# Soft-MoE over sigmoid attention on one core: the last six score units in halves of 224 queries, and attention's buffers in one tile

## Chip, cores and metric

One core of a Trainium2 chip runs the whole program. The metric is device microseconds from launch to end. Each number of a run is that of one execution; three executions of the kernel before were timed, and one more was profiled.

## What is computed

Attention with a sigmoid in place of the softmax, and then a mixture of experts in which every expert gets four "slots" that are soft mixtures of all tokens:

```
# q, k, v: (8, 12, 448, 64) fp32
attn = sigmoid(q @ k^T / 8 - log(448))
x = (attn @ v) as (3584, 768)          # tokens x model
logits = x @ phi                        # (3584, 32): 8 experts x 4 slots
d = softmax(logits, over the tokens);  slots = d^T @ x        # (32, 768)
slot_out[e] = relu(slots[e] @ w1[e]) @ w2[e]   # w1 (8,768,1024), w2 (8,1024,768)
out = softmax(logits, over the slots) @ slot_out               # (3584, 768)
```

The weights w1 and w2 are 50 MB, q, k and v 33 MB, the output 11 MB; all pass through one core's DMA.

## The kernel before

**Attention.** Two heads make a pair; there are 48 pairs, and their work is cut into 168 units (`seq`): for an even pair units (p, 0) to (p, 3), for an odd one (p, 0) to (p, 2). A unit (p, c) with c under 3 takes 128 keys; the unit (p, 3) takes the last 64 keys of p and of p+1. `score` (L267) writes the unit's scores of both heads, 128 x 2 x 448, into a PSUM tile `sc` (two banks, one for each head; two such tiles take turns) with TensorE (PE), and then ScalarE (ACT) takes the sigmoid of all 896 columns into one of three buffers `att` (L285). `weigh` (L295) multiplies V with it into the sums `av` (L318; for the last pair by two column parts, L293). In step i of the main loop (L606) PE gets `score` of unit i, then `weigh` of unit i - 2. `evac_a` (ACT, L321) and `evac_b` (DVE, L325) carry finished sums to x, `evac_last` (L327) those of the last pair, by two copies of DVE. PE, ACT, DVE and the DMA queue on SP each run their instructions in the order of the program, written out by hand; waits come from the tiles' uses.

**Loads.** SP's queue issues all loads. `load_qk`, `load_v`, `load_vl` bring a pair's Q and K, its V and the V of the odd 64 keys into buffers that must have come free. In between, `load` (L145) brings weights in units of 384 KB (128 x 768 fp32) into the places that `slots` (L108) lists. After attention's buffers come `wpe`, `wpx`, the tiles `wc1` to `wc6` of a second pool `wpb`, which lies where attention's buffers `qk`, `v` and `att` were, then `wpy`, and then the tiles `wa`, whose first contents PE has to read first (L190, the first product with w1).

**End of attention.** An ACT instruction on one element of the last sigmoid's buffer (L628, `dmx`) loads the table for exp early. PE computes the logits of the last pairs (L360), turns three pairs' x (L354), DVE and ACT take the last softmax (L499 to L509), PE sums the slots (L440; the first two of these sums read `wpy`), and then goes through w1 (L190) and w2 (L822); the output rows leave at the end.

Of the kernel before, what the change touches and what calls it, by code (L numbers as in the profile page):

```python
# [18 lines left out]
P = 128  # L19
NFK = 3  # L20
LAG = 2
PACE = 1.25
# [11 lines left out]
N_C = 6  # L34
# [34 lines left out]
def soft_moe_attention(ctx: ExitStack, tc: tile.TileContext, qk, v, vl, phi, w, wq, w8, wz, cst, out):  # L69
# [28 lines left out]
    state = {"next": 0, "ring": 0, "used": 0, "room": 0, "wpb": None, "n8": 0, "call": 0}  # L98
# [3 lines left out]
    wk = wpa.tile([P, UNIT + HALF], F32, name="wk")  # L102

# [4 lines left out]
    slots = wa_slots[:n1] + [(wpy, 0, 0, 2)] + wa_slots[n1:] + [(wpe, 0, 0, 4), (wpx, 0, 0, 2)]  # L108
    slots += [("wc", n, 0, 1) for n in range(1, N_C)] + [("wc", N_C, 0, 2), (wpy, 0, 2, 4)]
    slots += wa_slots + [(wpe, 0, 0, 4), (wpx, 0, 0, 2), (wpy, 0, 0, 4)] + wa_slots  # L110

    def ring_tile(size=1):
        while state["used"] + size > state["room"]:
            pool, n, used, room = slots[state["ring"]]
            state.update(ring=state["ring"] + 1, used=used, room=room)
            if pool == "wa":
                pool = wpa.tile([P, room * UNIT], F32, name=f"wa{n}")
            elif pool == "wc":
                pool = state["wpb"].tile([P, room * UNIT], F32, name=f"wc{n}")
# [9 lines left out]
    def load_half():  # L129
        state["wh"] = wk[:, UNIT:]  # L130
        nc.sync.dma_start(wk[:, UNIT:], wz[0][:, 0:HALF])

    def load_wk():
        utile[units[N_K]] = wk[:, 0:UNIT]
        nc.sync.dma_start(wk[:, 0:UNIT], w[N_K // 2][:, N_K % 2 * UNIT:(N_K % 2 + 1) * UNIT])
# [58 lines left out]
    with ExitStack() as actx:  # L194
        ap = actx.enter_context(tc.tile_pool(name="ap", bufs=1))

        kinds = {"qk": [P, QW], "v": [P, NFK, P], "att": [P, 2, S]}

        def hold(kind, n=""):
            if kind == "qk" and n == 0:  # L200
                return wk[:, 0:QW]
            return ap.tile(kinds[kind], F32, name=f"{kind}{n}")
# [53 lines left out]
        def load_v(p):  # L256
            if p < NP:
                t = get("v", p % 2)
                nc.sync.dma_start(t[:], v[p])
                vts[p] = t  # L260
# [6 lines left out]
        def score(u):  # L267
            p, c = u
            if u == seq[2]:
                sc = [ps_av.tile([P, 512], F32, name=f"av1{h}") for h in range(2)]  # L270
            else:
                tile2 = ps_sc.tile([P, 2, 512], F32, name="sc")
                sc = [tile2[:, h, :] for h in range(2)]
            for t in range(2):
                pt, k0 = (p, c * P + t * 64) if c < NFK else (p + t, NFK * P)
                for h, r in enumerate(heads):
                    nc.tensor.matmul(  # L277
                        sc[h][64 * t:64 * t + 64, 0:S], qkts[pt][r, S + k0:S + k0 + 64], qkts[pt][r, 0:S],
                        start=True, stop=True)
            att = get("att", seq.index(u) % 3)  # L280
            if u == seq[2]:
                for h in range(2):
                    nc.scalar.activation(att[:, h, :], sc[h][:, 0:S], AF.Sigmoid, bias=nbias, scale=QSCALE)
            else:
                nc.scalar.activation(att[:], tile2[:, :, 0:S], AF.Sigmoid, bias=nbias, scale=QSCALE)  # L285
            atts[u] = att

        parts = (slice(0, 2 * P), slice(2 * P, S))

        def weigh_half(o, w, att, start, stop):  # L290
            for k, t in enumerate(parts):
                for h, r in enumerate(heads):
                    nc.tensor.matmul(o[k][r, 0:t.stop - t.start], w[:, r], att[:, h, t], start=start, stop=stop)  # L293

        def weigh(u):  # L295
# [6 lines left out]
            if p == NP - 1:  # L302
                weigh_half(avs[p], vts[p][:, c, :], att, False, c == NFK - 1)
                return
            for t in range(2):
                row = slice(64 * t, 64 * t + 64)
                if c == NFK and p + t == NP - 1:
                    weigh_half(avs[p + t], vls[p // 2][row, :], att[row], True, False)
                    continue
# [17 lines left out]
        def evac_last(p):  # L327
            x, av = x_of(p), avs.pop(p)
            for k, t in enumerate(parts):
                nc.vector.tensor_copy(x[:, t], av[k][:, 0:t.stop - t.start])  # L330
# [153 lines left out]
        def last_job(b, lgt, pw, px):  # L484
# [8 lines left out]
            for c0 in (0, 2):  # L493
                logits(lg, b, [NPR - 1], (0, 1, 2, 3), c0, c0 + 2)
# [110 lines left out]
        for i in range(len(seq) + LAG):  # L605
            for f in early.get(i, ()):  # L606
                f()
            if i < len(seq):
                u = seq[i]
                score(u)  # L610
# [12 lines left out]
            if i == len(seq) - 1:  # L623
                lgt = ps_sc.tile([P, 2, 512], F32, name="sc")
                keep(1, lgt)
                logits_old(lgt[:, 0, :])
# [4 lines left out]
            if i >= LAG:  # L631
                u = seq[i - LAG]
                weigh(u)
                p, c = u
                if c == NFK:
                    evac_b(p)
                    load_vl(p // 2 + 1)
                elif c == NFK - 1:
                    load_v(p + 2)
                    if p == NP - 1:  # L640
                        work(B * S)
                        pw = ps_av.tile([P, 512], F32, name="av00")
                        px = [ps_av.tile([P, 512], F32, name="av01")]
                        pxt = ps_sc.tile([P, 2, 512], F32, name="sc")
                        keep(0, pxt)
                        px += [pxt[:, 0, :], ps_av.tile([P, 512], F32, name="av10")]
                        continue
                    evac_a(p)
                    if p == NP - 3:
                        todo.append((0.65, lambda p=p: evac_b(p)))  # L650
                    elif p % 2 == 1:
                        evac_b(p)
            for f in late.get(i, ()):
                f()
            work(rate.get(i, PACE))
        finish, ph0 = last_job(B - 1, lgt, pw, px)

    state["wpb"] = ctx.enter_context(tc.tile_pool(name="wpb", bufs=1, reuse_waits="tile"))
# [86 lines left out]
    def combine_turn(n, c4):  # L745
# [8 lines left out]
        while at0 < t0 + nt:  # L754
            i, m = divmod(at0, UNIT)
            w = min(UNIT - m, t0 + nt - at0)
            if m == 0:
                cts[i] = state["wpb"].tile([P, UNIT], F32R, name=f"wc{i + 1}")[:]
# [76 lines left out]
    wc_last = state["wpb"].tile([P, 2 * UNIT], F32R, name=f"wc{N_C}")[:]  # L835
# [83 lines left out]
```

## Time and profile before

| | us |
|---|---|
| median of three runs | 369.77 (369.0 to 369.96) |
| the profiled execution's own time | 370.01 |
| its span (first to last instruction) | 368.2 |
| PE busy in the span | 347.4 (94%) |
| ACT, DVE busy | 222.5 (60%), 242.3 (66%) |

Moved by DMA: 95.21 MB. The time of a run lies some 2 us above the span. A busy time is a union: matmuls that overlap in the array count once. The profile's chain of waits goes back from the last instruction, at each step to what released it; the views in time order show when one instruction starts, how long it takes and how many of its kind follow each other (an fp32 matmul shows as two records). Times within the span are counted from its start.

### The profile page before, as it was taken

To read this page: it belongs to the slowest core of one execution; us is meant where nothing else is said; L and a number is where in the kernel's file an instruction comes from. 1 tells how busy PE (TensorE), PEld (TensorE's weight loads), DVE (VectorE), ACT (ScalarE), POOL (GpSimd) and SP (SyncE) were. 2 spreads that over 40 slices of the span, in tenths; PEclk is the share of its full clock that TensorE was granted. 3 is DMA by queue.
4 is the path that set the end of the run, shared out by engine and by line. 5 is a ranking of instruction groups with operands and counts; after the bars stand their busy time and mean duration, and the time that the engine had idled before them with its cause. 6 is when DMAs were issued, how large, how long until landed. Compare 5 with 4: busy or idle time off the path is not lost.

```text
span 368.2 us, 10407 instructions
## 1 busy us (share of the span) xinstructions
PE 347.4 (94%) x4341; PEld 177.0 (48%) x4341; DVE 242.3 (66%) x621; ACT 222.5 (60%) x307; POOL 10.1 (3%) x45
## 2 busy tenths in 40 slices
PE   9999999999999999999999999999999999699840
PEld 5666666644444446444444644464546553243620
DVE  0148829796795886869958695979955784123650
ACT  5777777577777774777777387758582114322640
POOL 1000000000000000000000000010103001000000
PEclk9999999999999999999999999999999999989985
DMA  6766666465676663666666387729899999999997
GB/s 216 228 211 206 195 225 203 157 215 173 209 228 214 200 189 113 217 210 208 196 215 209 101 280 259 271 72 350 292 334 349 417 441 426 411 426 402 384 412 281
DMA packets 34783, 95.21 MB, mean 259 GB/s; under 512 B 3632, under 2 KB 17584, under 8 KB 33328
## 3 DMA queue, kind: packets, MB, share of 16 engines
q1 hardware_dynamic: 34736, 94.55, 73.0%
q8 instruction: 34, 0.56, 0.6%
q14 instruction: 13, 0.11, 0.1%
HBM read 83.53 MB, written 11.01 MB: 257 GB/s over the span
## 4 chain that ended last, share of the span: by engine, by line
PE 80%; DMA 14%; DVE 2%; ACT 0%; issue 0%; ACTq 0%; DVEq 0%; SPq 0%
PE sc L277 35%; PE av L318 34%; DMA wpe<-in_wq_dram 9%; DMA wa<-in_w_dram 5%; PE sc L440 2%; PE av L190 2%; PE sc L378 2%; DVE wa L769 1%; PE av L768 1%; PE sc L360 1%; PE av L557 1%; PE pt L768 1%; PE av L293 1%; PE av L822 0%; PE av L440 0%
## 5 line engine op out<-in xcount | busy, mean ns | idle before, releaser
L285 ACT ACTIVATE att<-sc,sm 128x896 f32<-128x896 f32 x167 | 167.7, 1007 | 76.8 <-PE sc L277 73.6
L318 PE MATMUL av<-att,v 64*64 64x448 f32 x1128 | 140.3, 536 | 0.0
L277 PE MATMUL sc<-qk 64*64 64x448 f32 x896 | 118.4, 537 | 0.0
L318 PEld LDWEIGHTS av<-att,v 64*64 64x64 f32 x1128 | 51.0, 133 | 55.9 <-issue 46.3
L277 PEld LDWEIGHTS sc<-qk 64*64 64x64 f32 x896 | 41.7, 133 | 43.6 <-issue 29.6
L277 PE MATMUL sc<-wk 64*64 64x448 f32 x440 | 62.4, 546 | 0.0
L342 DVE STREAM_TRANSPOSE wa<-wpe 32x384 f32<-32x384 f32 (+5 forms) x144 | 58.0, 403 | 2.2
L342 DVE STREAM_TRANSPOSE wa<-xy 32x192 f32<-32x192 f32 (+3 forms) x96 | 33.1, 345 | 1.6
L325 DVE TENSOR_TENSOR wpe<-wpe,av 128x448 f32<-128x448 f32 x18 | 11.2, 621 | 31.8 <-PE av L318 20.6
L277 PEld LDWEIGHTS sc<-wk 64*64 64x64 f32 x440 | 21.3, 136 | 21.5 <-issue 15.1
L342 DVE STREAM_TRANSPOSE wa<-wpx 32x288 f32<-32x288 f32 (+1 forms) x48 | 24.9, 520 | 0.8
L822 PE MATMUL av<-wa,hw 128*32 128x384 f32 x208 | 21.1, 507 | 3.6 <-DMA wa<-in_w_dram 3.6
L318 PE MATMUL av<-att,wk 64*64 64x448 f32 x188 | 23.9, 536 | 0.0
L325 DVE TENSOR_TENSOR wpx<-wpx,av 128x448 f32<-128x448 f32 x15 | 9.3, 621 | 18.0 <-PE av L318 15.7
L190 PE MATMUL av<-wa,phi 128*32 128x256 f32 x312 | 17.6, 380 | 0.4 <-DVE phi L522 0.4
L325 DVE TENSOR_TENSOR xy<-xy,av 128x448 f32<-128x448 f32 x14 | 8.7, 622 | 9.4 <-ACT xy L321 3.8
L769 DVE COPY wa<-pt 128x384 f32<-128x384 f32 x23 | 11.9, 555 | 3.2 <-PE pt L768 2.8
L769 ACT COPY wa<-av 128x384 f32<-128x384 f32 x23 | 10.6, 479 | 4.7 <-PE av L768 4.0
L318 PEld LDWEIGHTS av<-att,wk 64*64 64x64 f32 x188 | 8.7, 133 | 9.5 <-issue 8.0
L190 PEld LDWEIGHTS av<-wa,phi 128*32 128x32 f32 x312 | 9.6, 110 | 7.3 <-DVE tmp L712 0.9
L715 ACT COPY t<-tmp 128x32 f32<-128x32 f32 x8 | 1.7, 218 | 17.5 <-DVE tmp L713 17.5
L342 DVE STREAM_TRANSPOSE wpe<-xy 32x256 f32<-32x256 f32 (+3 forms) x32 | 11.0, 344 | 0.5
(189 smaller groups left out, 287.2 us busy)
## 6 DMA issues: line engine op xcount, KB each, us to landing
wa<-in_w_dram SPq DMA_DIRECT2D x52, 384.0 KB, 4.1
qk<-in_qk_dram SPq DMA_DIRECT2D x32, 448.0 KB, 3.7
v<-in_v_dram SPq DMA_DIRECT2D x48, 192.0 KB, 2.6
wa<-in_wq_dram SPq DMA_DIRECT2D x6, 1536.0 KB, 31.3
wa<-in_w_dram SPq DMA_DIRECT2D x3, 3072.0 KB, 23.0
wk<-in_qk_dram SPq DMA_DIRECT2D x15, 448.0 KB, 3.4
out_dram<-wa SPq DMA_DIRECT2D x13, 384.0 KB, 7.4
out_dram<-wa SPq DMA_DIRECT2D x2, 1536.0 KB, 7.6
```

What stands on the lines that cost most here:

```text
L190: nc.tensor.matmul(ph[32 * j:32 * j + 32, 0:256], phi_sb[:, kc, :], wt, start=(kc == 0), stop=(kc == NKC - 1))
L277: nc.tensor.matmul(sc[h][64 * t:64 * t + 64, 0:S], qkts[pt][r, S + k0:S + k0 + 64], qkts[pt][r, 0:S], start=True, stop=True)
L285: nc.scalar.activation(att[:], tile2[:, :, 0:S], AF.Sigmoid, bias=nbias, scale=QSCALE)
L293: nc.tensor.matmul(o[k][r, 0:t.stop - t.start], w[:, r], att[:, h, t], start=start, stop=stop)
L318: nc.tensor.matmul(o[t][r, 0:S], w, att[row, h, :], start=start, stop=stop)
L325: nc.vector.tensor_tensor(out=x_of(p), in0=x_of(p), in1=av[0][:, 0:S], op=ALU.add)
L342: nc.vector.transpose(y[32 * g:32 * g + 32, k0:k0 + n, c0:c0 + m, BLK * a:BLK * a + BLK], src)
L378: nc.tensor.matmul(lg[32 * j:32 * j + 32, BLK * c0[j]:BLK * (c0[j] + n)], phi_sb[:, hp, :], blocks(x, j if x is xa else (j + 2) % 4, n), s ...
L440: nc.tensor.matmul(sls[t][32 * a:32 * a + 32, BLK * k0:BLK * k1], zt[:, c * BLK:(c + 1) * BLK], y_of(t, gi, c)[:, k0:k1, BLK * a:BLK * a + ...
L768: nc.tensor.matmul(pf[:, 0:HALF], ct_of(m, t, n), sts[hf], start=True, stop=True)
L769: (nc.scalar.copy, nc.vector.tensor_copy)[k % 2](ov, pf[:, 0:HALF])
L822: nc.tensor.matmul(po[32 * fl:32 * fl + 32, 0:HALF], h[:, k:k + NSLOT], w2_chunk(hf, e, g, fl), start=(n == 0), stop=(n == 2 * E - 1))
```

## The change

- The last six units, (46, 1) to (47, 2), go by halves of 224 queries. Half j = 2m or 2m + 1 belongs to unit m of these six. `score_half` writes both halves of a unit into one PSUM tile `sc`, columns 0:224 and 224:448 of each head's bank, and takes one sigmoid for each half, 128 x 2 x 224, into one of three buffers of 448 columns (`halves`) in place of 896. `weigh_half` uses one half. In a step PE now gets score 2m, weigh 2m - 2, score 2m + 1, weigh 2m - 1.
- All of attention's buffers but `qk0` and the last sums lie at written-out places in one tile `big` (7 units and 128 columns), and the weights that were in `wc1` to `wc6` go there by units, in the order 0, 3, (wpx), 1, 2, 6, 5, 4. The tile of two units, `wc6`, becomes two loads.
- V of the last two pairs goes into `xy`, to the columns where these pairs' x is put later. The V of the odd keys moves from `wk` into `big`, and the half unit of `load_half` is loaded with `load_wk`, eight places earlier in SP's queue.
- `evac_last` gives the second 224 columns to ACT in place of DVE, and the logits of the last pair are cut to fit.

```diff
+        halves = [big[:, a:a + S].rearrange("p (h s) -> p h s", h=2) for a in (at_att0 + S, at_att0, at_att1 + S)]
...
+                if p >= NP - 2:
+                    a = (p % 2 + 1) * NBK * P
+                    t = xy[:, a:a + nv].rearrange("p (c f) -> p c f", c=NFK)
+                nc.sync.dma_start(t, v[p])
...
+        parts = (slice(0, S // 2), slice(S // 2, S))
+        sc_half = [None]
+
+        def score_half(j):
+            (p, c), k = seq[len(seq) - N_HALF + j // 2], j % 2
+            if k == 0:
+                sc_half[0] = ps_sc.tile([P, 2, 512], F32, name="sc")
+            sc = sc_half[0][:, :, parts[k]]
+            for t in range(2):
+                pt, k0 = (p, c * P + t * 64) if c < NFK else (p + t, NFK * P)
                 for h, r in enumerate(heads):
+                    nc.tensor.matmul(
+                        sc[64 * t:64 * t + 64, h, :], qkts[pt][r, S + k0:S + k0 + 64], qkts[pt][r, parts[k]],
+                        start=True, stop=True)
+            nc.scalar.activation(halves[j % 3], sc, AF.Sigmoid, bias=nbias, scale=QSCALE)
...
-            for k, t in enumerate(parts):
-                nc.vector.tensor_copy(x[:, t], av[k][:, 0:t.stop - t.start])
+            for k, copy in enumerate((nc.vector.tensor_copy, nc.scalar.copy)):
+                copy(x[:, parts[k]], av[k][:, 0:S // 2])
...
-            if i == len(seq):
-                nc.scalar.activation(dmx[0:1, :], atts[seq[-1]][0:1, 0, 0:1], AF.Exp)
+            else:
+                nc.scalar.activation(dmx[0:1, :], halves[(2 * N_HALF - 1) % 3][0:1, 0, 0:1], AF.Exp)
...
+            if i > n0:
+                weigh_half(2 * (i - n0) - 2)
+                if i < len(seq):
+                    score_half(2 * (i - n0) + 1)
...
+                weigh_half(2 * (i - n0) - 1)
+                weighed(seq[i - 1])
+            elif i >= LAG:
+                weigh(seq[i - LAG])
+                weighed(seq[i - LAG])
+                if i == n0:
+                    score_half(1)
+                    weigh(seq[i - 1])
+                    weighed(seq[i - 1])
...
-    for k, size in enumerate((1, 1, 1, 1, 1, 1, 1, 2, 2)):
-        if k == N_C + 1:
+    for k, size in enumerate((1, 1, 1, 1, 1, 1, 1, 1, 1, 2)):
+        if k == 7:
             load_kept()
-        if k == 4:
-            load_half()
         load(size)
```

PE, the last units of attention, before: scores are L277, weighing L293, `Activation` in brackets is a wait for ACT.

```order
L277 MATMUL sc<-qk_3035 64x448 [waits Activation_49]
L277 MATMUL sc<-qk_3035 64x448 x3
L293 MATMUL av_3231<-att_3217,v_3178 64x256 [waits DMAHW3_49]
L293 MATMUL av_3231<-att_3217,v_3178 64x256
L293 MATMUL av_3232<-att_3217,v_3178 64x192 x2
L293 MATMUL av_3231<-att_3229,v_3178 64x256 [waits Activation_49]
```

The same place now: scores are L303, weighing L315.

```order
L303 MATMUL sc<-big 64x224 [waits PE_49]
L303 MATMUL sc<-big 64x224 x3
L315 MATMUL av_3002<-big,xy 64x224 x2
L303 MATMUL sc<-big 64x224 [waits Activation_49]
L303 MATMUL sc<-big 64x224 x3
L315 MATMUL av_3003<-big,xy 64x224 x2
L315 MATMUL av_3002<-big,xy 64x224 x2
L315 MATMUL av_3003<-big,xy 64x224 [waits Activation_49]
```

Of each unit the second half's scores wait for ACT, and the weighing that follows them needs no wait of its own. Before, the score of a unit waited for the sigmoid of the unit two steps back. In the built program the wait of the second half's first matmul has the count of one certain ACT instruction: the sigmoid of the same unit's first half.

ACT at the end of attention, before: L285 is the sigmoid, L628 the early exp, L501 belongs to the last softmax.

```order
L285 ACTIVATE att_3245<-sc,sm 128x896 [waits PE_49,Activation_49]
L628 ACT_TABLE_LOAD
L628 ACTIVATE sm<-att_3245 1x1 [waits Activation_49]
L501 COPY sm<-sm 32x1 [waits DVE_49,Pool_49]
L504 COPY sm<-sm 32x1 [waits DVE_49]
```

And now: L306 is a half's sigmoid, L358 the copy of `evac_last`.

```order
L349 COPY xy<-av_2945 128x448 [waits DMAHW6_49,PE_49]
L306 ACTIVATE big<-sc,sm 128x448 [waits PE_49,Activation_49] x6
L670 ACT_TABLE_LOAD
L670 ACTIVATE sm<-big 1x1 [waits Activation_49]
L358 COPY xy<-av_3003 128x224 [waits DMAHW4_49,DVE_49,PE_49]
L530 COPY sm<-sm 32x1 [waits DVE_49,Pool_49]
```

The copy of the last sums to x stands on ACT, behind the table load, which stands behind the last half's sigmoid.

SP's queue from the second load of `wpe` on, before.

```order
L172 DMA wpe<-in_w_dram 128x1536 [waits DVE_49,DMAHW2_49,PE_49,Pool_49]
L259 DMA v_3178<-in_v_dram 128x384 [waits DMAHW3_49,PE_49]
L172 DMA wpx<-in_w_dram 128x768 [waits DMAHW4_49,DVE_49]
L172 DMA wpx<-in_w_dram 128x768 [waits DMAHW5_49]
L172 DMA wc_3413<-in_w_dram 128x768 [waits DMAHW6_49,PE_49]
L172 DMA wc_3415<-in_w_dram 128x768 [waits DMAHW7_49,PE_49]
```

And now, from the same place to `wpy`.

```order
L169 DMA wpe<-in_w_dram 128x1536 [waits DVE_49,DMAHW3_49,PE_49,Pool_49]
L263 DMA xy<-in_v_dram 128x384 [waits DMAHW4_49]
L169 DMA big<-in_w_dram 128x768 [waits DMAHW5_49,PE_49]
L169 DMA big<-in_w_dram 128x768 [waits DMAHW6_49,PE_49,Activation_49]
L169 DMA wpx<-in_w_dram 128x768 [waits DMAHW7_49,DVE_49]
L169 DMA wpx<-in_w_dram 128x768 [waits DMAHW0_49]
L169 DMA big<-in_w_dram 128x768 [waits DMAHW1_49,PE_49]
L169 DMA big<-in_w_dram 128x768 [waits DMAHW2_49]
L169 DMA big<-in_w_dram 128x768 [waits DMAHW3_49,PE_49]
L127 DMA lt<-in_wz_dram 128x768 [waits DMAHW4_49,DVE_49]
L169 DMA big<-in_w_dram 128x768 [waits DMAHW5_49,PE_49,Activation_49]
L169 DMA big<-in_w_dram 128x768 [waits DMAHW6_49,PE_49,Activation_49]
```

V of the last pair no longer waits for PE, and two weight units stand ahead of `wpx`. The next row in both is the load of `wpy`, which waits for PE and GpSimd (POOL) in both; what has been loaded by then is the same set.

## Rows read from the trace of the kernel before

**Rows 1.** The chain of waits, in order of time: start us, us, what.

```profile
288.48 18.28 DMA wa<-in_w_dram
...
306.82 33.15 DMA wpe<-in_wq_dram
...
341.71 0.49 ACT tmp L795
...
342.25 0.61 PE av L806 x2
```

**Rows 2.** Busy time by stretches: us, engines, granted clock, DMA share, GB/s.

```profile
264.00:276.00 12.00, 12.00 (x132) 5.76 (x131) 7.72 (x20) 8.87 (x10) 1.30 (x5) 1.00 0.90 308
276.00:280.00 4.00, 3.90 (x116) 3.28 (x112) 2.73 (x13) 2.43 (x10) 1.57 (x6) 1.00 0.94 305
...
288.00:300.00 12.00, 12.00 (x224) 6.82 (x220) 9.92 (x38) 1.86 (x8) 0.21 (x1) 1.00 1.03 434
310.00:320.00 10.00, 7.84 (x73) 2.96 (x73) 2.26 (x8) 4.67 (x12) 0.84 (x4) 1.00 0.98 415
320.00:325.00 5.00, 3.56 (x22) 1.42 (x22) 1.12 (x2) 0.59 (x2) 0.21 (x1) 0.78 1.01 423
```

**Rows 3.** SP's queue in time order, 263 to 286 us: start, us, issue.

```profile
263.89 0.83 SPq L172 DMA_DIRECT2D wpe<-in_w_dram  x2
267.17 0.33 SPq L259 DMA_DIRECT2D v<-in_v_dram  x1
...
276.55 0.51 SPq L172 DMA_DIRECT2D wc<-in_w_dram  x1
280.12 0.33 SPq L172 DMA_DIRECT2D wpy<-in_w_dram  x1
280.71 1.58 SPq L168 DMA_DIRECT2D wa<-in_wq_dram  x3
284.15 1.62 SPq L172 DMA_DIRECT2D wa<-in_wq_dram  x2
```

**Rows 4.** DMA issues of the page: count, KB each, median us from issue to landing.

```profile
wk<-in_vl_dram SPq DMA_DIRECT2D x24, 64.0 KB, 2.2
wpe<-in_w_dram SPq DMA_DIRECT2D x2, 768.0 KB, 4.7
...
wpy<-in_w_dram SPq DMA_DIRECT2D x1, 768.0 KB, 6.7
```

**Rows 5.** PE in time order, 265 to 277 us: start, us, matmuls.

```profile
265.43 0.93 PE L277 MATMUL sc<-qk 64*64 64x448 f32 x8
266.18 0.93 PE L318 MATMUL av<-att,v 64*64 64x448 f32 x8
...
272.63 0.50 PE L293 MATMUL av<-att,wk 64*64 64x192 f32 x4
272.94 0.94 PE L277 MATMUL sc<-qk 64*64 64x448 f32 x8
273.81 2.49 PE L293 MATMUL av<-att,v 128*64 128x256 f32 x24
```

**Rows 6.** ACT in time order, 266 to 277 us.

```profile
266.49 1.01 ACT L285 ACTIVATE att<-sc,sm 128x896 f32<-128x896 f32 x1 [0.50 <-PE sc L277]
...
274.00 1.01 ACT L285 ACTIVATE att<-sc,sm 128x896 f32<-128x896 f32 x1 [0.50 <-PE sc L277]
275.03 1.28 ACT L628 ACT_TABLE_LOAD   x1
276.32 0.20 ACT L628 ACTIVATE sm<-att 1x1 f32<-1x1 f32 x1
```

**Rows 7.** ACT line 283, the two sigmoids of 448 columns near the start: min/median/max ns.

```profile
L283 ACT ACTIVATE att<-av,sm x2: 634/638/642, 7.3 to 7.8; 128x448 f32<-128x448 f32 x2
```

**Rows 8.** DVE in time order, 275 to 280 us.

```profile
276.02 0.69 DVE L330 COPY xy<-av 128x256 f32<-128x256 f32 x2 [0.19 <-PE av L293]
277.19 0.29 DVE L499 CUSTOM_DVE_ANT_0 t<-sc,t 128x128 f32<-128x128 f32 x1 [0.47 <-PE sc L360]
```

More of the change, by code (lines that the diff above doesn't have):

```diff
@@ L21 @@
 LAG = 2
+N_HALF = 6
 PACE = 1.25
@@ L97, in soft_moe_attention @@
     N_SEQ = len(units) - 2
-    state = {"next": 0, "ring": 0, "used": 0, "room": 0, "wpb": None, "n8": 0, "call": 0}
+    state = {"next": 0, "ring": 0, "used": 0, "room": 0, "n8": 0, "call": 0}
     utile, quads = {}, {}
@@ L107, in soft_moe_attention @@
     n1 = 3 + (n1 - 3) // 2
-    slots = wa_slots[:n1] + [(wpy, 0, 0, 2)] + wa_slots[n1:] + [(wpe, 0, 0, 4), (wpx, 0, 0, 2)]
-    slots += [("wc", n, 0, 1) for n in range(1, N_C)] + [("wc", N_C, 0, 2), (wpy, 0, 2, 4)]
+    slots = wa_slots[:n1] + [(wpy, 0, 0, 2)] + wa_slots[n1:] + [(wpe, 0, 0, 4), (big, 0, 0, 1), (big, 0, 3, 4)]
+    slots += [(wpx, 0, 0, 2)] + [(big, 0, n, n + 1) for n in (1, 2, 6, 5, 4)] + [(wpy, 0, 2, 4)]
     slots += wa_slots + [(wpe, 0, 0, 4), (wpx, 0, 0, 2), (wpy, 0, 0, 4)] + wa_slots
@@ new lines, in weigh_half @@
+        def weigh_half(j):
+            (p, c), k = seq[len(seq) - N_HALF + j // 2], j % 2
+            att, q = halves[j % 3], parts[k]
+            if c == NFK and k == 0:
+                avs[p + 1] = [ps_av.tile([P, 512], F32, name=f"av1{t}") for t in range(2)]
+            if p == NP - 1:
+                for h, r in enumerate(heads):
+                    nc.tensor.matmul(
+                        avs[p][k][r, 0:S // 2], vts[p][:, c, r], att[:, h, :], start=False, stop=c == NFK - 1)
+                return
+            for t in range(2):
+                row = slice(64 * t, 64 * t + 64)
+                for h, r in enumerate(heads):
+                    if c < NFK:
+                        o, w, stop = avs[p][t][r, q], vts[p][row, c, r], c == NFK - 1 and t == k == 1
+                    elif t == 0:
+                        o, w, stop = avs[p][0][r, q], vls[p // 2][row, r], k == 1
+                    else:
+                        o, w, stop = avs[p + 1][k][r, 0:S // 2], vls[p // 2][row, r], False
+                    nc.tensor.matmul(o, w, att[row, h, :], start=c == NFK and t == 1, stop=stop)
@@ L603, in work, with weighed @@
                 n -= k
-        for i in range(len(seq) + LAG):
+        def weighed(u):
+            p, c = u
+            if c == NFK:
+                evac_b(p)
+                load_vl(p // 2 + 1)
+            elif c == NFK - 1 and p < NP - 1:
+                load_v(p + 2)
+                evac_a(p)
+                if p == NP - 3:
+                    todo.append((0.65, lambda p=p: evac_b(p)))
+                elif p % 2 == 1:
+                    evac_b(p)
+        n0 = len(seq) - N_HALF
+        for i in range(len(seq) + 1):
             for f in early.get(i, ()):
@@ L609, in soft_moe_attention @@
                 u = seq[i]
-                score(u)
+                if i < n0:
+                    score(u)
+                else:
+                    score_half(2 * (i - n0))
                 if u[1] == NFK:
@@ L833, in soft_moe_attention @@
     h_part(*prev)
[L835 removed]
+    big = big_at(F32R)
+    wc_last = big[:, 5 * UNIT:7 * UNIT]
     c4s = {}
```

95 lines of the change are left out of this document (35 added, 60 removed).

## The prediction

> **What bounds the kernel now.** I read the chain of waits first. From 288.48 us to 339.97 us it is nothing but two transfers of weights, 18.28 and 33.15 us from issue to landing [rows 1]: the end is set by the DMA. The stretches show where that begins [rows 2]. From 288 to 300 us the share is 1.03 at 434 GB/s, and at 310 to 325 us still 415 to 423. From 264 to 276 us it is 0.90 at 308 GB/s, and PE is busy for the whole of it. So from somewhere past 280 us on the chip moves bytes as fast as they go, and the time is set by how many are left then and by whether the stream breaks. Ahead of that the loads wait for buffers.
>
> SP's queue says for which [rows 3]. The loads of `wpe` to `wc6` go out from 263.89 to 276.55 us, 14 of them, 5760 KB (5.90 MB). Then SP waits to 280.12 us, until PE has read `wpy` for the last time in the slot sums; the loads into `wa` behind it follow PE at 280.71 and 284.15 us. In 264 to 280 us 4.92 MB went (12 x 308 and 4 x 305), so some 0.98 MB were still queued when `wpy` came. This cushion is why the 3.5 us without an issue cost nothing. Whatever moves the issue of `wpy` by more than the cushion breaks the stream, and everything behind it is late.
>
> **What the change does on PE.** The columns stay the same, and so does array time: the part of unit (46, 3) that was already in 256 and 192 columns fits the usual rhythm, 272.63 to the next score at 272.94 us [rows 5]; more weight loads cost nothing there, and I take nothing. What is new is a wait. The order shows that the scores of a unit's second half wait for ACT, and the built program says for which instruction: the sigmoid of the first half, just ahead. Before, PE waited for a sigmoid two units back.
>
> The price of one such wait, from S, the start of the first half's scores:
> - a score of a unit holds PE for 0.75 us (265.43 to 266.18) and ends after 0.93, so its tail is 0.18 [rows 5]; a half issues for 0.375 and ends at S + 0.555;
> - the sigmoid began at 266.49, 0.13 after the scores ended at 266.36 [rows 5, 6]: S + 0.685;
> - a sigmoid of 448 columns took 0.638 us [rows 7], 896 took 1.01 [rows 6]: it ends at S + 1.32;
> - PE followed ACT after 0.05 us at 342.20 to 342.25 [rows 1]: S + 1.37.
>
> Between the two halves PE has one weighing of a half, so without the wait it would go on at S + 0.75. The loss is 0.62 us in each of five units, 3.1 us. In the first of the six a whole weighing (0.75) stands between, so it loses 0.25. The last weighing waits for the last sigmoid behind two halves of weighing, another 0.25. The sums of pair 46 are copied by ACT ahead of a sigmoid, 0.1 (estimate: the copy starts 0.31 after a half's scores do and holds ACT some 0.4, against 0.685). Sum 3.7 us. Bounds: with the sigmoid at half of 1.01 and half the lag of 0.13, the half scores' answer is at S + 1.17, the loss 0.42 for five and 0.05 for two, 2.2 us; with a half's sigmoid as dear as a whole one it is 1.0 and 0.6, 6.2 us. I stay with 3.7, because its row has the very size.
>
> **The end of attention.** Before, the last sigmoid ended at 275.01, the table load ran under PE's weighing until 276.31, and DVE copied the last sums 276.02 to 276.71 [rows 6, 8]; the weighing ended at 276.30 [rows 5], so x was whole 0.41 us behind it. Now the last sigmoid ends only 0.60 us ahead of the end of weighing (0.05, then 0.375 and 0.18), and ACT's queue is sigmoid, table load 1.28, exp 0.20, copy. With 0.35 for the copy (half of DVE's 0.69) and 0.03 of gaps x is whole 1.86 us behind the sigmoid, 1.26 behind the weighing. That is 0.85 us later; the chain from there through DVE's step at 277.19 to the slot sums has the same links. Bounds 0.6 and 1.1. The Trainium skill (ScalarE: Activation LUTs, What ACT_TABLE_LOAD costs) gives the load 1.28 us and a drain of 1.38 us behind it; the row has the 1.28, but the exp began 0.01 us after it, so the trace shows no drain here. By the page this term would be 2.2 and the whole change 1.4 us dearer.
>
> **What comes earlier.** V of pair 47 need not wait for 267.17 any more, and four units of weights can start in 267 to 271 us, where three of them stood among the loads up to 276.55. This fills gaps (share 0.90). But `wpy` stands behind them, all loads ahead of it are the same bytes, and they are through before it comes, so the early start is worth only what it takes out of the cushion, and only if `wpy` is not late. The one load more (`wc6` in two) and the moves of V and the half unit in SP's queue are costed at nothing: the queue is waiting, not issuing, there. The first 162 units wait for the same things as before.
>
> **The sum.** `wpy` is released 3.7 + 0.85 = 4.55 us later. The cushion takes part of it. `wpy` landed 6.7 us after its issue, `wpe` of the same size 4.7 [rows 4]: by this it stood 2.0 us behind others. By bytes 0.98 MB at about 0.41 is 2.4 us, less the time that a transfer needs to begin, which lies between 0 and the 2.2 us of a 64 KB load [rows 4]: 0.2 to 2.4. I take 1.6, nearer to the landings. The stream breaks for 4.55 - 1.6 = 2.95 us. Behind it nothing gives this back, since the share is 0.98 to 1.03 there [rows 2]. Nor is more lost: `wpy` and the three `wa` loads behind it (2304 KB, some 5.7 us) keep the stream full from about 286 to 291.9 us, and the next two `wa` loads come at 284.15 + 4.55 = 288.7 [rows 3]; and PE, 1.6 us later against the stream than before, has 2.16 us of idle time in 310 to 320 and 1.44 us in 320 to 325 [rows 2]. The profiled execution took 370.01, 0.24 above the median of 369.77; on its own time the sum is 372.96. I forecast 372.7 for the median.
>
> **The rivals.**
> - *The early loads decide, faster.* If PE's wait were hidden (its place: the second half's scores; ACT fast enough, or the wait not in the way), `wpy` would be 0.85 late, less than the cushion, and with all earlier bytes through, the stream gains 1.6 - 0.85 = 0.75 us: 369.0; with the copy hidden too, 368.2. It decides for a gain as soon as `wpy` comes less than 1.6 us late. For it: the share of 0.90. Against: the wait stands in the order, and 1.37 cannot go into 0.75. Chance 0.13, more than half of it beyond 0.3% (1.1 us, about what a measurement of this kernel can tell from no change).
> - *The wait is short and the cushion long, no change.* 2.2 + 0.6 - 2.4 = 0.4: 370.2. Against it is the row of 0.638 us. Chance 0.12.
> - *The clock falls.* The halved units keep PE busy 1.5 of 2.12 us, 71%. In 320 to 325 us PE was busy 3.56 of 5 us, 71%, and the granted clock was 0.78, between the levels; in 310 to 320 us it was busy 78% at 1.00 [rows 2]. At half clock a unit's PE work takes 3.0 us, and with a wait left of some 0.25, 3.25 instead of 2.12: over three units 3.4 us more, 376.1. The Trainium skill (TensorE: Matmul & The Clock Gate, Part 1: The HAM clock gate) says that the array's clock is halved when PE has been idle; which gaps did it in 320 to 325 no row here tells apart. Gaps of 0.6 us are short, so chance 0.07.
> - *Doesn't do what it says.* The order shows both halves and the new places; none of this is in doubt.
>
> **The numbers.** Forecast case 0.68; its own ends are 370.2 (2.2 + 0.6 less 2.4) and 374.5, where a wait of 0.75 makes 4.5 of 3.7, the copy is 1.1 and the cushion 0.9. Range 370.1 to 374.5: it leaves out the faster rival and most of the clock's. Slower by over 0.3%: 0.68 + 0.07 + 0.02 = 0.77; within: 0.05 from the first rival and 0.10 from the second, 0.15; faster 0.08.
>
> **What would show it.** PE at 266 to 280 us: idle ahead of every second half's scores, ended by ACT, 0.5 to 0.65 us in five units, and weighing ending near 280.0 instead of 276.30. ACT: table load behind the last half's sigmoid, the copy ending 1.2 to 1.3 us behind the weighing. SP: `wpy` issued near 284.7 instead of 280.12, and landing after 4.5 to 5 us instead of 6.7. The share of the DMA low (0.4 to 0.8) somewhere in 276 to 286 us, and as before from 290 on. I am wrong if PE does not wait there, or if it does and the stream does not break because more is queued than I count, or if weighing slows by itself under the doubled weight loads.

## The result, and the profile after

The changed kernel takes **373.97 us** (median of five runs, 373.33 to 374.35) beside 369.77 for the kernel before on the same chip: ratio 1.0108, 95% interval 1.0079 to 1.0138. It is slower, by 4.2 us; the forecast was 372.7 in a range of 370.1 to 374.5. Of the runs further down, two executions, of 928.24 and 525.09 us, are left out of the medians.

The two profiled executions are compared from one row that the change doesn't touch, the first of the two loads into `wpe`: 263.89 us before [rows 3], 264.38 after. What lies ahead of it differs by some tenths from one execution to the next (263.76 in a second profile of the changed kernel), so "later" below means later against that row, 0.49 us less than the plain difference of times.

The stretches say where the time went: span of the stretch, busy time of PE, PEld, DVE, ACT and POOL, granted clock, DMA share, GB/s. First the kernel before, over stretches that its rows above did not group like this:

```profile
264.00:288.00 24.00, 23.50 (x394) 13.67 (x397) 15.03 (x52) 12.02 (x22) 4.58 (x17) 1.00 0.94 333
...
300.00:325.00 25.00, 21.40 (x231) 8.86 (x227) 10.26 (x35) 8.53 (x24) 1.88 (x9) 0.96 1.00 423
```

The same view after, first in whole and then the part that matters in pieces of 2 us:

```profile
264.00:288.00 24.00, 21.04 (x388) 12.10 (x378) 12.12 (x40) 13.11 (x26) 2.72 (x11) 1.00 0.76 268
288.00:300.00 12.00, 11.96 (x218) 7.05 (x218) 9.11 (x33) 1.65 (x7) 2.07 (x8) 1.00 1.02 409
300.00:325.00 25.00, 23.08 (x309) 10.53 (x301) 13.50 (x50) 8.79 (x26) 1.69 (x8) 1.00 1.00 426
...
276.00:278.00 2.00, 1.71 (x24) 0.61 (x20) 0.12 (x1) 1.18 (x2) 0.00 (x0) 1.00 0.44 173
278.00:280.00 2.00, 1.72 (x24) 0.73 (x18) 1.24 (x5) 0.80 (x2) 0.00 (x0) 1.00 0.00 0
280.00:282.00 2.00, 1.91 (x36) 0.89 (x32) 1.02 (x2) 1.97 (x4) 0.00 (x0) 1.00 0.57 147
282.00:284.00 2.00, 1.74 (x22) 1.65 (x23) 0.96 (x6) 0.82 (x4) 0.36 (x2) 1.00 0.68 204
284.00:286.00 2.00, 1.92 (x81) 1.38 (x83) 1.62 (x8) 1.31 (x6) 0.94 (x3) 1.00 0.95 363
286.00:288.00 2.00, 1.64 (x52) 1.07 (x44) 0.87 (x5) 0.00 (x0) 0.12 (x1) 1.00 0.78 274
```

From 264 to 288 us the DMA's share fell from 0.94 to 0.76, 4.3 us of transfers in 24; from 288 us on it is full as it was [rows 2]. The loss is a hole in the stream of weights, and it lies wholly in this stretch. The hole has two parts: from 276 to 284 us the shares leave 4.6 us of transfers unused (nothing at all moves from 278 to 280), and there is a smaller gap of 0.4 us at 286. PE, idle for 0.5 us of the stretch before, now idles 3.0.

PE in time order shows why. L303 is the scores of a half, L327 and L315 the weighing of a half (L315 is the last pair); columns are start, us, line, operation, shape, count, and in brackets the idle time ahead and what ended it:

```profile
265.91 0.56 PE L303 MATMUL sc<-big 64*64 64x224 f32 x8
...
267.28 0.61 PE L303 MATMUL sc<-big 64*64 64x224 f32 x8
...
268.46 0.56 PE L303 MATMUL sc<-big 64*64 64x224 f32 x8
268.84 0.56 PE L327 MATMUL av<-big,xy 64*64 64x224 f32 x8
269.83 0.61 PE L303 MATMUL sc<-big 64*64 64x224 f32 x8 [0.44 <-ACT big L306]
270.26 0.56 PE L327 MATMUL av<-big,xy 64*64 64x224 f32 x8
270.64 0.56 PE L303 MATMUL sc<-big 64*64 64x224 f32 x8
...
275.23 0.56 PE L303 MATMUL sc<-big 64*64 64x224 f32 x8
275.72 0.60 PE L315 MATMUL av<-big,xy 128*64 128x224 f32 x4
276.60 0.61 PE L303 MATMUL sc<-big 64*64 64x224 f32 x8 [0.29 <-ACT big L306]
277.14 0.60 PE L315 MATMUL av<-big,xy 128*64 128x224 f32 x4
277.67 0.61 PE L303 MATMUL sc<-big 64*64 64x224 f32 x8
278.21 0.60 PE L315 MATMUL av<-big,xy 128*64 128x224 f32 x4
279.09 0.61 PE L303 MATMUL sc<-big 64*64 64x224 f32 x8 [0.28 <-ACT big L306]
279.63 1.48 PE L315 MATMUL av<-big,xy 128*64 128x224 f32 x12
```

The second half's scores start 1.37 us behind the first's (265.91 to 267.28, 268.46 to 269.83, 275.23 to 276.60): the wait on the sigmoid, row after row. And from 275.72 us on there is something else: scores and weighing follow each other after 0.53 us where nothing waits (277.14, 277.67, 278.21), and not after 0.375 as at 268.46 and 268.84. The weighing ends at 281.11 us, 4.32 later than 276.30 [rows 5].

ACT at that end, in time order:

```profile
279.83 0.63 ACT L306 ACTIVATE big<-sc,sm 128x448 f32<-128x448 f32 x1 [0.79 <-PE sc L303]
280.48 1.28 ACT L670 ACT_TABLE_LOAD   x1
281.78 0.20 ACT L670 ACTIVATE sm<-big 1x1 f32<-1x1 f32 x1
281.89 0.32 ACT L358 COPY xy<-av 128x224 f32<-128x224 f32 x1
```

The copy of the last sums starts behind the table load. DVE in time order, with the copy of `lt` for which SP waits:

```profile
280.50 0.63 DVE L622 COPY sc<-lt 128x448 f32<-128x448 f32 x1 [1.07 <-ACT big L306]
281.16 0.39 DVE L358 COPY xy<-av 128x224 f32<-128x224 f32 x1
```

x is whole at 282.21 us, 1.10 behind the weighing where it was 0.41 [rows 5, 8]. SP's queue in time order:

```profile
264.38 0.83 SPq L169 DMA_DIRECT2D wpe<-in_w_dram  x2
...
267.28 1.79 SPq L169 DMA_DIRECT2D big<-in_w_dram  x2
269.41 0.80 SPq L169 DMA_DIRECT2D wpx<-in_w_dram  x2
272.65 7.44 SPq L169 DMA_DIRECT2D big<-in_w_dram  x3
281.15 0.33 SPq L127 DMA_DIRECT2D lt<-in_wz_dram  x1
281.58 0.85 SPq L169 DMA_DIRECT2D big<-in_w_dram  x2
285.58 0.33 SPq L169 DMA_DIRECT2D wpy<-in_w_dram  x1
```

and SP's waits from 262 to 290 us: who waits, for whom, us in total, times, longest:

```profile
SPq L169 <- PE sc L303: 8.7, 2, 6.2
...
SPq L127 <- DVE sc L622: 1.0, 1, 1.0
```

`wpy` goes out 4.97 us later, and lands 4.9 us after its issue, not 6.7 [rows 4]. But it is not the only late load. The last of the three units issued from 272.65 us on stands 6.2 us at the head of the queue, because its place holds Q and K until the last scores have read them; with it wait `lt` and two units more. All these went out by 276.55 before [rows 3]. The chain's last two links start 5.46 and 3.60 us later by the plain times, but are transfers as before:

```profile
293.94 16.42 DMA wa<-in_w_dram
...
310.42 33.38 DMA wpe<-in_wq_dram
```

### The profile page after: what moved, and what is told of

Read it like the earlier page. It is cut to its first block, busy times and chain, and to the rows that moved or that the text cites. A ratio compares the mean times of both kernels' runs of the same rounds, so it can differ in the third digit from the quotient of the medians.

```text
span 372.4 us, 10548 instructions
## 1 busy us (share of the span) xinstructions
PE 350.0 (94%) x4409; PEld 169.9 (46%) x4409; DVE 242.4 (65%) x620; ACT 224.4 (60%) x314; POOL 10.1 (3%) x45
## 4 chain that ended last, share of the span: by engine, by line
PE 75%; DMA 16%; ACT 2%; DVE 2%; issue 1%; SPq 0%; ACTq 0%; DVEq 0%
PE sc L281 32%; PE av L346 32%; DMA wpe<-in_wq_dram 9%; DMA wa<-in_w_dram 4%; PE sc L468 2%; PE sc L406 2%; PE av L187 2%; DMA big<-in_qk_dram 2%; DMA big<-in_w_dram 1%; DVE wa L809 1%; PE sc L303 1%; PE av L808 1%; ACT big L306 1%; PE pt L808 1%; PE sc L388 1%
## 5 line engine op out<-in xcount | busy, mean ns | idle before, releaser
L289 ACT ACTIVATE big<-sc,sm 128x896 f32<-128x896 f32 x161 | 161.7, 1007 | 75.1 <-PE sc L281 72.1
L346 PE MATMUL av<-big 64*64 64x448 f32 x1288 | 174.2, 536 | 0.0
L281 PE MATMUL sc<-big 64*64 64x448 f32 x848 | 121.2, 537 | 0.1
L346 PEld LDWEIGHTS av<-big 64*64 64x64 f32 x1288 | 61.5, 133 | 62.4 <-issue 60.4
L281 PE MATMUL sc<-wk 64*64 64x448 f32 x440 | 65.9, 540 | 0.0
L281 PEld LDWEIGHTS sc<-big 64*64 64x64 f32 x848 | 41.4, 133 | 48.3 <-issue 39.4
L306 ACT ACTIVATE big<-sc,sm 128x448 f32<-128x448 f32 x12 | 7.6, 635 | 5.5 <-PE sc L303 5.0
L799 ACT CAST big<-sc 128x512 fp32r<-128x512 f32 (+5 forms) x11 | 4.5, 433 | 9.1 <-PE sc L790 9.1
```

What stands on the lines that cost most here:

```text
L281: nc.tensor.matmul(sc[h][64 * t:64 * t + 64, 0:S], qkts[pt][r, S + k0:S + k0 + 64], qkts[pt][r, 0:S], start=True, stop=True)
L289: nc.scalar.activation(att, tile2[:, :, 0:S], AF.Sigmoid, bias=nbias, scale=QSCALE)
L306: nc.scalar.activation(halves[j % 3], sc, AF.Sigmoid, bias=nbias, scale=QSCALE)
L346: nc.tensor.matmul(o[t][r, 0:S], w, att[row, h, :], start=start, stop=stop)
```

## The experiments

The runs below ask five questions: what the wait costs by itself; what the buffers and the order of loads do by themselves; how much lateness of `wpy` the stream bears; whether the slower rhythm of the last pair is the alternation of tile shapes; and whether the copy on ACT or the loads behind the last weighing count. A time is a median, with its ratio to the kernel before beside it on the same chip (369.66 to 369.80) and the 95% interval. The ratio is not the quotient of the two medians; the two can differ by 0.1%.

**The halves in PSUM tiles of their own.**

```diff
-            if k == 0:
-                sc_half[0] = ps_sc.tile([P, 2, 512], F32, name="sc")
-            sc = sc_half[0][:, :, parts[k]]
+            sc = ps_sc.tile([P, 2, 512], F32, name="sc")[:, :, 0:S // 2]
```

> The changed kernel with one edit: every half writes its scores into a PSUM tile of its own, columns 0:224, so that the second half's scores no longer wait for the sigmoid of the first half. The halves, the buffers, the places and the loads stay. Theory (the wait makes the loss): the gaps of 0.5 to 0.85 us ahead of the second halves' scores go, the weighing ends 3 to 3.5 us earlier than in the changed kernel (near 277.8 instead of 281.1), wpy is issued near 282.2 instead of 285.58, and the time is 370.2 to 371.0 us. Rival 1 (the halved matmuls themselves are slow, by weight loads or by changes of the tile's shape): most of the gap stays, 372.8 to 374. Rival 2 (the new places and the order of the loads make the loss): 373 to 374.

Measured 370.96 us, ratio 1.0037 (1.0019 to 1.0055): 3.0 us of the 4.2 are gone with the wait. PE in the last pair, where no scores wait any more:

```profile
271.66 0.56 PE L325 MATMUL av<-big 64*64 64x224 f32 x8
272.12 0.61 PE L301 MATMUL sc<-big 64*64 64x224 f32 x8
272.66 0.60 PE L313 MATMUL av<-big,xy 128*64 128x224 f32 x4
273.19 0.61 PE L301 MATMUL sc<-big 64*64 64x224 f32 x8
...
275.87 1.48 PE L313 MATMUL av<-big,xy 128*64 128x224 f32 x12
```

Up to 271.66 us a half follows a half after 0.375 us. From 272.12 us on, where the scores are on 64 x 64 tiles and the weighing on 128 x 64, it takes 0.53 to 0.54, for seven steps: 7 x 0.16 = 1.1 us. The weighing ends at 277.35, 1.24 later than before (this execution's `wpe` row is 0.19 early). One wait is left: the last three pieces take 1.48 us, as in the changed kernel, because the last one waits for the last sigmoid (estimate: 0.18 us, 1.48 less three times 0.375 and a tail of 0.18). The rest has no wait to explain it.

The Trainium skill (PSUM — Partial Sum Buffer, PSUM bank collisions) has a rule that bears on this: guard PSUM by bank and group of partitions, not by address, since a TensorE write into a bank while ScalarE uses the same partitions of it is an error, at other columns too. The second half's columns are free, its bank isn't. That fits the wait in the program, and its going with another tile, so with other banks. But waits come from the tiles' uses, and the run changes tile and bank together, so it does not tell which of the two the wait is for; writing into the same bank without the wait was not tried.

**The buffers and loads alone, units whole.** The change's tile `big`, V in `xy` and the loads by units, with `score`, `weigh` and `evac_last` as before; of the two units that the change loads ahead of `wpx`, unit 0 alone goes there:

```diff
-    slots = ... + [(wpe, 0, 0, 4), (big, 0, 0, 1), (big, 0, 3, 4)]
-    slots += [(wpx, 0, 0, 2)] + [(big, 0, n, n + 1) for n in (1, 2, 6, 5, 4)] + [(wpy, 0, 2, 4)]
+    slots = ... + [(wpe, 0, 0, 4), (big, 0, 0, 1)]
+    slots += [(wpx, 0, 0, 2)] + [(big, 0, n, n + 1) for n in (1, 6, 5, 4, 3, 2)] + [(wpy, 0, 2, 4)]
```

> The buffers' part of the change alone: all of attention's buffers in one tile, V of the last two pairs in the place of their sums, the half unit and the last weight units moved ahead, but the last six units whole, with three sigmoid buffers of 896 columns, and the last sums copied by DVE alone. Since the sigmoid buffers come free later, the weight units go to the tile in the order 0, (wpx), 1, 6, 5, 4, 3, 2. Theory: no new wait on PE, weighing ends within 0.5 us of 276.3, wpy is issued at 280.1 to 280.6, and as the loads ahead of it are the same bytes the time is 369.0 to 370.0. Rival 1 (halved matmuls): the same. Rival 2 (places and load order): 372 to 374.

Measured 369.46 us, ratio 0.9989 (0.9974 to 1.0004): no difference that can be told. `wpy` goes out at 280.02 us and lands after 6.9, as before. The new places cost nothing that shows by themselves, and the earlier loads give nothing that shows.

**The kernel before, with `wpy` late.** Extra matmuls of 128 x 128 into an unused PSUM tile, ahead of the slot sums, when the loads ahead of `wpy` have gone out: 14 of them, and 5.

```diff
-            warm(pw, 2)
+            warm(pw, 16)
```

> The kernel before, with 14 more matmuls of 128 x 128 on the identity in PE's queue just ahead of the last slot sums: about 3.1 us of delay (0.22 us each) between the end of attention and the release of wpy, and nothing else. They change no output. Theory (a stream of loads with a cushion of 1.3 to 1.6 us): wpy near 283.2, the time 371.2 to 371.7. Rival (no cushion, every delay of PE there passes in full): 372.7 to 373.0. Rival (the end is not set there): 369.5 to 370.0.

> The same with 5 more matmuls, about 1.1 us of delay. Theory (cushion of 1.3 to 1.6 us): 369.5 to 370.1, no change. Rival (no cushion): 370.7 to 371.0.

With 14, `wpy` goes out 2.95 us later and the time is 371.25 us, ratio 1.0031 (1.0016 to 1.0047): 1.45 us for 2.95 (0.6 to 1.7 by the interval), so by the time the stream bears 1.5 us (1.2 to 2.4). With 5 it is 0.94 later, and 370.11 us, ratio 1.0007 (0.9989 to 1.0025), is no measurable change. So there is a cushion in the kernel before, as the prediction had it. That lateness beyond it is paid in full is what both runs fit, not what they show: one point lies beyond it.

**The same two delays with the change's loads.** On the kernel with whole units, 14 matmuls once ahead of the slot sums, and once ahead of the last weighing:

```diff
+                if i == len(seq) + 1:
+                    warm(lgt[:, 0, 2 * P:3 * P], 14)
                 weigh(u)
```

> Whole units, with the change's buffers and order of loads (369.46), and 14 more matmuls of 128 x 128 ahead of the slot sums: wpy 2.95 us late, nothing ahead of it. Theory A (the early loads fill gaps but by 280 us the same bytes have gone, so as much is queued ahead of wpy as before the change): cost 1.45 us as with the kernel before, 370.7 to 371.2. Theory B (the early loads took the cushion away): cost 2.4 to 2.95 us, 371.9 to 372.4.

> Whole units as the one before, but the 14 matmuls stand ahead of the last weighing: the end of attention is 2.95 us late, and with it the loads behind it (lt and the last two units of weights) and wpy. Theory A (with the early loads the queue is empty when attention ends, so what delays attention's end delays the stream in full): cost 2.5 to 2.95 us, 371.9 to 372.4, with a share of the DMA under 0.3 for over 1.5 us somewhere in 275 to 280 us. Theory B (only wpy's lateness counts, where it breaks the stream): the same time as the kernel with the matmuls ahead of the slot sums, within 0.3 us.

Ahead of the slot sums: 371.02 us, ratio 1.0035 (1.0022 to 1.0048), 1.56 over whole units for 2.96 of lateness; the early loads did not take this cushion away, as the first theory had it. Ahead of the last weighing: 371.94 us, ratio 1.0051 (1.0038 to 1.0064), 2.48 over whole units. SP's queue there (the `wpe` row is at 264.75):

```profile
276.90 0.38 SPq L127 DMA_DIRECT2D lt<-in_wz_dram  x1
280.71 0.81 SPq L169 DMA_DIRECT2D big<-in_w_dram  x2
284.44 0.33 SPq L169 DMA_DIRECT2D wpy<-in_w_dram  x1
```

`lt` went out on time (12.15 us behind the `wpe` row, 12.14 with whole units); the two units are 3.3 us late. The time is 0.92 more than with the matmuls ahead of the slot sums, but they took more there (3.32 us between weighing and weighing), and `wpy` is 3.47 late, not 2.96, against whole units. 0.5 of the 0.92 is that; the 0.4 that is left is inside the two intervals. Nor did the share fall under 0.3 for 1.5 us ahead of `wpy`: it was 0.66 in 280 to 282 us. The direction is that of the first theory; the size is not shown.

**Fewer changes of tile shape.** Own tiles, both copies of the last sums on DVE, and then also the halves grouped, scores, scores, weighing, weighing, with a fourth half buffer and the weights of unit 3 loaded last:

```diff
-            for k, copy in enumerate((nc.vector.tensor_copy, nc.scalar.copy)):
+            for k, copy in enumerate((nc.vector.tensor_copy, nc.vector.tensor_copy)):
```

> The halves in PSUM tiles of their own, and both copies of the last sums on DVE. Theory (the stream is broken twice, ahead of the loads behind the last weighing and ahead of wpy, and the copy behind ACT's table load makes only wpy late): x is whole about 0.7 us behind the weighing instead of 1.1, wpy is issued 0.3 to 0.5 us earlier than in the kernel with own tiles alone (281.81 us), and the time is 0.2 to 0.5 us below its 370.96: 370.5 to 370.8. Rival 1 (wpy's lateness is all that counts): 0.5 below, 370.4 or less. Rival 2 (the first break alone sets the loss): 371.0, no difference.

```diff
                     score_half(2 * (i - n0))
+                    if i > n0:
+                        score_half(2 * (i - n0) + 1)
...
                 weigh_half(2 * (i - n0) - 2)
-                if i < len(seq):
-                    score_half(2 * (i - n0) + 1)
```

> As the one before, with the two halves' scores of a unit in a row, then the two weighings of the unit before, four half buffers, and the weights of unit 3 loaded last. Theory (a change of tile shape costs PE about 0.16 us, and what it delays is paid by the stream): half as many changes in the last pair, the weighing ends at 276.5 to 276.9 us instead of 277.35, and the time is 369.4 to 370.3. Rival 1 (the shape is free, and the slow cadence of the last pair comes from something that goes with the halves): it ends at 277.2 or later, time 370.5 to 371. Rival 2 (ACT, with two sigmoids of 0.64 us for each 1.5 us of PE, holds it up): idle time of PE that ACT ends, 0.1 to 0.3 us in each unit, time above 371.

The copies alone: 371.15 us, ratio 1.0038 (1.0026 to 1.0051), no different from 370.96. The trace says why: DVE's first copy starts at 278.38 us, behind its copy of `lt`, and x is whole 1.11 us behind the weighing, as it was with ACT. The edit did not remove the term that it was meant to remove. Grouped: 370.25 us, ratio 1.0026 (1.0009 to 1.0043), and PE in the last pair:

```profile
272.60 0.99 PE L301 MATMUL sc<-big 64*64 64x224 f32 x16
273.54 0.98 PE L313 MATMUL av<-big,xy 128*64 128x224 f32 x8
274.45 0.99 PE L301 MATMUL sc<-big 64*64 64x224 f32 x16
275.37 1.73 PE L313 MATMUL av<-big,xy 128*64 128x224 f32 x16
```

Two halves of one kind take 0.75 us, and the next kind starts after 0.91 to 0.94: again about 0.17 for a change, now with half as many changes. The weighing ends at 277.10 us, 0.48 later than before where own tiles alone had 1.24. On the clock of the kernel with own tiles this end is 276.59 us (its `wpe` row is 0.51 earlier), inside the 276.5 to 276.9 that was expected, and so is the time. PE is nowhere idle for ACT in the halves, and the last weighing does not wait for it either, so some 0.2 of the 0.76 gained is that wait. The rest goes with the number of changes: the cost goes with the change of shape, not with the halves.

**The copy of the last sums, and the loads behind `lt`.** In the changed kernel, both copies on DVE and ahead of its second copy of `lt`:

```diff
+        evac_last(NP - 1)
         pw = ps_av.tile([P, 512], F32, name="av00")
...
         keep(0, pxt)
...
-            evac_last(p)
```

> The changed kernel with both copies of the last sums on DVE and ahead of the second copy of lt into PSUM: x is whole some 0.7 us earlier (0.4 behind the weighing instead of 1.10) and wpy goes out near 284.9 us instead of 285.58, but the copy of lt, and with it the load into lt and the two units of weights that stand behind it in SP's queue, come 0.7 to 1.0 us later than 281.15 and 281.58. Theory (the loads behind the last weighing find an empty queue; most of the loss is the break ahead of them): no gain, 373.8 to 374.7, and the DMA's dry stretch grows by 0.7 to 1.0 us. Rival (wpy's issue beyond a fixed cushion sets the time): 0.6 to 0.7 us less, 373.2 to 373.4.

```profile
281.96 0.33 SPq L127 DMA_DIRECT2D lt<-in_wz_dram  x1
282.39 0.85 SPq L169 DMA_DIRECT2D big<-in_w_dram  x2
284.76 0.33 SPq L169 DMA_DIRECT2D wpy<-in_w_dram  x1
```

`wpy` goes out 0.53 us earlier than in the changed kernel and `lt` 1.1 later (the `wpe` row is at 264.09). The time is 373.24 us, ratio 1.0100 (1.0075 to 1.0124): 0.73 less than 373.97, as the rival had it, though the intervals overlap. So both kernels ran once more, side by side:

> The changed kernel once more, beside the next one on one chip: 373.9, within 0.3 us.

> The kernel with both copies of the last sums on DVE ahead of the second copy of lt once more. Theory (the two breaks of the stream trade one for one: lt and the units behind it 1.1 us later, wpy 0.5 us earlier): the same as the changed kernel beside it within 0.3 us. Rival (wpy's issue alone sets the time): 0.5 to 0.8 us less, with intervals that part.

Now 373.46, ratio 1.0101 (1.0082 to 1.0119; 373.9 was expected), and 373.08, ratio 1.0088 (1.0068 to 1.0109): 0.38 less, again with overlapping intervals. Each pair alone decides nothing. The mean of the two differences is 0.55, which would be `wpy`'s 0.53, with nothing for the 1.1 us of the loads behind `lt`.

Last, the same on the grouped kernel, with the load of `lt` behind the two units:

```diff
-        if k == 7:
+        if k == 9:
             load_kept()
```

> The grouped halves with tiles of their own, both copies of the last sums on DVE and ahead of the second copy of lt, and the load into lt moved behind the two units of weights. Theory (the loads behind the last weighing are not held by lt any more, and x is whole 0.4 to 0.5 us behind the weighing instead of 1.55): wpy 0.5 to 1.1 us earlier than 282.03, the share of the DMA in 276 to 280 us not below the 0.88 of the grouped kernel, time 369.3 to 369.9, the same as before the change within 0.3%. Rival (what is left of the loss lies in PE's later weighing alone): 370.2 as the grouped kernel.

`wpy` came 0.57 us earlier than in the grouped kernel, and the time did not follow: 370.76 us, ratio 1.0035 (1.0017 to 1.0053), where 369.3 to 369.9 was expected. The share in 276 to 280 us was 0.68, and 0.88 in the grouped kernel. By the time this speaks against the reading just made, but the interval overlaps the grouped kernel's, and the profiled execution took 370.21 us. No version with halves beat the kernel before, and whole units only equal it.

All runs by two measures: how late `wpy` is issued against the `wpe` row, what the time is above the kernel before it ran beside, and what the first leaves over the second. The last two columns take bytes in place of times. They say how much less the profiled execution had moved since the span's start than that of the kernel before, at the same distance behind the `wpe` row (the mean of five places 28 to 44 us behind it), and what lateness is left over that at 0.42 MB/us [rows 2].

| kernel | `wpy` late, us | cost, us | difference | behind, MB | difference by bytes, us |
|---|---|---|---|---|---|
| whole units | 0.0 | -0.34 | | 0.05 | |
| before, 5 matmuls | 0.94 | 0.31 | 0.6 | 0.06 | 0.8 |
| grouped, copies first | 1.02 | 1.08 | -0.1 | 0.14 | 0.7 |
| grouped | 1.59 | 0.55 | 1.0 | 0.30 | 0.9 |
| own tiles | 1.88 | 1.16 | 0.7 | 0.36 | 1.0 |
| own tiles, DVE copies | 1.91 | 1.44 | 0.5 | 0.47 | 0.8 |
| before, 14 ahead of the slot sums | 2.95 | 1.45 | 1.5 | 0.85 | 0.9 |
| whole units, 14 ahead of the slot sums | 2.95 | 1.31 | 1.6 | 0.80 | 1.0 |
| whole units, 14 ahead of the weighing | 3.46 | 2.23 | 1.2 | 1.09 | 0.9 |
| changed, copies first (two runs) | 4.44, 4.44 | 3.56, 3.42 | 0.9, 1.0 | 1.48, 1.50 | 0.9, 0.9 |
| changed (two runs) | 4.97, 4.98 | 4.20, 3.80 | 0.8, 1.2 | 1.70, 1.83 | 0.9, 0.6 |

By the times the cushion seems to be 1.5 to 1.6 where only `wpy` is late, and 1.2 or less where attention's end is late too. But an interval of these costs is 0.5 to 1.1 us to either side, and by the ratios the grouped kernel would cost 0.96 and whole units with 14 ahead of the weighing 1.89, so this is a hint at most.

The bytes, of one execution each, do not bear it out: by them the cushion is 0.6 to 1.0 us in every kernel, and 0.9 and 1.0 where only `wpy` is late. The loss follows `wpy`'s lateness, us for us beyond that, and no run shows that other late loads add to it. Where the hole lies differs (in the changed kernel 0.88 of the 1.70 MB are missing 18 us behind the row already, in the kernel before with 14 matmuls nothing), but what the cushion takes does not. Copies first, with `wpy` 0.53 us earlier and `lt` 1.1 later, lose 0.22 and 0.33 MB less, 0.5 and 0.8 us; on the grouped kernel it is 0.16 MB, 0.4 us for 0.57. Times and bytes need not agree, because between some 340 and 365 us nearly all these executions, late or not, move 0.2 to 0.4 MB more than that of the kernel before.

## Why the prediction was right, and where it was not

**The end is the DMA's, through a late `wpy`: right.** The stretch 264 to 288 us holds the loss, and after it the stream is as full as before. The delay of 2.95 us put into the kernel before cost 1.45 by the time and 2.0 by the bytes, as a cushion would have it. (The loads of `wpe` to `wc6` are 13 and not the 14 that the prediction counts; its sum of bytes is right.)

**The wait: right in mechanism and to the hundredth in price.** S + 1.37 was forecast from the sigmoid of 0.638 us [rows 7], and 1.37 stands in the trace, in the first unit too. Its sum was taken too high, 3.7 us. In the first four units it is 0.62 twice and 0.85 once (272.82 to 274.42 us, where ACT's copy of the sums stands ahead: 0.23 and not 0.1), with 0.25 for the first; in the last two units only 0.30 and 0.35, since PE needs 1.07 there without any wait; and 0.18 at the end: 3.2 us. Own tiles keep the last 0.18 and take 3.1 us off the end of the weighing and 3.0 off the time.

**That "more weight loads cost nothing there, and I take nothing": this step failed.** It was argued from pieces of unit (46, 3), which are all on 64 x 64 tiles. The last pair's weighing is on 128 x 64, and before the change its 24 records, 12 matmuls, run in one piece behind the last scores [rows 5], with one change of shape. The halves make PE change at every piece, for 0.16 us each, 1.1 to 1.2 us in all. The hint stood in the rows: the score of 272.94 is followed by the weighing at 273.81, after 0.87 us and not 0.75 [rows 5]. With the wait's 3.2 it makes up the 4.32 us of the weighing's end, where 3.7 was forecast: two errors of opposite sign.

**The copy behind the table load: right, 0.69 for 0.85.** The weighing ended 0.65 behind the last sigmoid, not 0.60, and the copy took 0.32, not 0.35, starting 0.11 after the exp's start and not after its end. With the drain that the Trainium skill (ScalarE: Activation LUTs, What ACT_TABLE_LOAD costs) adds to the load, and which the prediction set aside, the copy could not have started at 281.89 us, 0.13 after the load of 1.28 had ended. The drain does not appear here either, nor ahead of the load, which starts 0.02 after the last sigmoid has ended.

**The cushion: right in kind, mis-sized.** 1.6 was taken. By the bytes it is 0.9 us in the changed kernel, 0.6 in its second run, and 0.9 in the kernel before with 14 matmuls, so it was too large from the start and not through the change; by the times it is 0.8, 1.2 and 1.5. The step that failed is "I take 1.6, nearer to the landings": the landings gave 2.0, and what was measured lies in the middle of the other estimate, 0.2 to 2.4. What the prediction did not see is that four of the loads ahead of `wpy`, the unit in the place of Q and K, `lt` and two units, wait for the same PE, so that the queue stood empty ahead of them for some 3 us. But that they "are through before it comes" holds: `lt` and the two units are 1.18 MB, 2.8 us at 0.42 MB/us (estimate), and `wpy` is issued 4.4 us behind `lt`, with a gap at 286 us. With the copies first it is issued 2.8 us behind `lt`, and the loads ahead are only just through. So no run shows that their lateness added to the loss, and none tests a `wpy` that comes sooner behind them.

**The sum.** Forecast 4.55 - 1.6 = 2.95; measured 4.97 - 0.8 = 4.2 (4.98 - 1.2 = 3.8 in the second set of runs), and by the bytes 4.0 and 4.4. Of the error of 1.25 us, 0.4 is `wpy` and 0.8 the cushion. The time lies in the range because its upper end allowed a shorter cushion of 0.9.

**The rivals.** The early loads did not decide: with whole units they gave 0.34 us, inside the interval. The wait was not short. The clock did not fall: 1.00, the higher of its two levels (2.4 GHz), was granted throughout 264 to 325 us, with PE idle 0.28 to 0.66 us at a time; the dip before the end (0.78 in 320 to 325 us before, 0.66 in 325 to 330 after) only moved with the rest.

## What to carry to other kernels

When a step is halved to make a pipeline finer, ask whether the second half's output lies in the buffer that the first half's consumer still reads: then the pipeline has lost a stage, and the price is the full round trip of one half, which rows of the old trace gave to a hundredth here. Look for a change of tile shape wherever an order alternates two kinds of matmul, and read its price from a place in the old trace where the shapes meet. And where a stream of loads sets the end, count the bytes that have moved by a fixed distance behind a row that the change doesn't touch, and not only the time at the end: over these kernels the times put the cushion anywhere from -0.1 to 1.6 us, and the bytes at 0.6 to 1.0.

## Not expected of the hardware

Matmuls of 64 x 64 tiles followed by 128 x 64 tiles, or the other way round, started 0.16 us later than matmuls of one shape (0.53 to 0.54 for a piece, where one of the same shape took 0.375; 0.91 to 0.94 for two pieces, where it took 0.75). It showed in all kernels with halves, and at the one such change in the kernel before (0.87 us in place of 0.75) [rows 5]. Grouping the pieces by shape brought the end of the weighing forward by 0.76 us, some 0.2 of it by a wait that went. After a wait on ACT, the piece that follows the scores also came 0.43 us behind them, not 0.375.
